# Attention scores: the keys' low parts on 64 rows of TensorE for each head, and one product for both heads in the last block

## The chip, the cores and the metric

The kernel runs on one core of a Trainium2 chip. The metric is the device time of one launch in microseconds (us). TensorE (PE) multiplies, VectorE (DVE), ScalarE (ACT) and GpSimd (POOL) do the elementwise work, SyncE (SP) issues most of the transfers.

## What is computed

Three stages follow one another: a causal attention with a decay, a mixture of four experts over all tokens, and a second mixture in which one of eight experts is picked for some of the tokens. The change is in the first.

```python
def _attn_ref(q, k, v, f):                 # q, k, v: (2, 8, 576, 64), f: (2, 8, 576)
    scores = scale * np.matmul(q, k.transpose(0, 1, 3, 2))
    log_f = np.log(np.clip(f, 0.0001, 1.0))
    cum = np.cumsum(log_f, axis=-1)
    decay = cum[:, :, :, None] - cum[:, :, None, :]
    scores = np.where(causal, -1000000000.0, scores + decay)
    attn = np.exp(scores - np.max(scores, axis=-1, keepdims=True))
    attn = attn / (np.sum(attn, axis=-1, keepdims=True) + 1e-09)
    return np.matmul(attn, v).astype(np.float32)
```

## The kernel before

**Split operands.** A score is made from rounded (fp32r) parts: a head's query q is its rounded value plus the rest, and so is its key k. The 64 features of a head fill only 64 of TensorE's 128 rows. So the host packs q twice, one copy under the other, and the kernel makes of one copy the high part and of the other the low part (`q_low`); the tile is `qa`. One product with the keys' high part `kh`, which also stands on both halves, then gives (q high + q low) times k high. The product of q high with k low needs only the 64 rows of q high. Before, it is run on all 128 rows: the tile `kl` of shape [128, 2, 576] has a head's low part on that head's rows, and zeros on the other 64, which are written once at the start.

**Pairs and steps.** The 16 heads are taken as 8 pairs (p = 0 to 7), and the 576 queries of a head as four blocks of 128 (i = 0 to 3) and a last one of 64, for which both heads of the pair share one block of 128 output rows (i = 4). A pair is thus five steps. `emit_s(p, i)` emits a step's scores: for each head h the product with `kh`, the one with `kl` and the causal mask (a product of a bf16 identity and `maskd`), all into one PSUM tile `s`. N, the columns of a product, is 256, 256, 384 and 512 for i = 0 to 3; block 4 has two halves of 288 columns. DVE then adds the decay and takes the minimum (`sn`, `mn`, L335, or L356 for block 4), ACT takes the exponential (`e`, L338).

**The order is written by hand.** The loop over `steps` (L633) emits for each n in this order: the transposes of the exponentials of step n-2 (`emit_tp`, tiles `tp`, copied to `et` by ACT for head 0 and by DVE for head 1), the scores of step n, for block 4 of the pair before the transposes of the reciprocals of the sums (`emit_rp`, tile `rp`, from `rsx` that ACT writes), and the products with v (`emit_av`, tiles `avm`, `avt`: both heads side by side on 64 columns of TensorE each). Products with v are emitted after the scores of steps i = 1 (28 products, of blocks 2 and 3 of the pair before), i = 2 (block 4 of the pair before) and i = 4 (12 products); after those of steps 0 and 3 the next loop turn's transposes follow at once. In the last two turns there are no scores left, and the first products of the next stage (`early_product`, tiles `p1_e`, `p6_e`, `p7_e`) are emitted among the last pair's remaining work.

**What ties the engines together.** Three PSUM tiles `s` go round. A step takes two, so the second head's tile of step n is the first head's of step n-1: PE waits there until DVE has read that. Each engine takes its instructions in the order in which they are emitted. The splits of the coming pairs (`split_k`: kh on DVE, kl on POOL; `split_q`: qa on DVE, the low part on POOL) are emitted between the steps.

Of the kernel before, what the change touches and what calls it, by code (L numbers as in the profile page):

```python
# [7 lines left out]
F32 = mybir.dt.float32  # L8
# [23 lines left out]
TOPAD = 640  # L32
QW = 2 * TOPAD
# [14 lines left out]
def kernel(  # L48
# [179 lines left out]
    with ExitStack() as at:  # L228
# [7 lines left out]
        ps_s = ps_p[0]  # L236
# [5 lines left out]
        kls = [spl_p.tile([P, 2, S], F32R, tag=f"kl{i}", name=f"kl_{i}", bufs=1) for i in range(2)]  # L242
# [30 lines left out]
        def first_loads():  # L273
            raw = raw_p.tile([P, QKW], F32, tag="raw", name="qk_0")
            state[0] = dict(raw=raw)
            for c0, c1 in ((0, CUT), (CUT, S)):
                for o, st, e in ((QW, S, 0), (0, TOPAD, TOPAD - S)):
                    c2 = c1 + e if c1 == S else c1
                    vw = [x[:, o:o + 2 * st].rearrange("p (h c) -> p h c", h=2)[:, :, c0:c2] for x in (raw, qk[0])]
                    SY.dma_start(out=vw[0], in_=vw[1])  # L280

# [7 lines left out]
        def split_k(p):  # L289
# [8 lines left out]
            for h in range(2):  # L298
                rows = slice(64 * h, 64 * h + 64)
                G.tensor_tensor(out=kl[rows, h], in0=rk[rows, h], in1=kh[rows, h].bitcast(F32), op=ALU.subtract)  # L300

        def q_low(p, h, eng):
            raw, qa = state[p]["raw"], state[p]["qa"]
            rows, cols = slice(64 - 64 * h, 128 - 64 * h), slice(TOPAD * h, TOPAD * h + TOPAD)
# [7 lines left out]
        def emit_s(p, i, between=lambda: None, gaps=None):  # L312
            st = state[p]
            qa, kh, kl, bi = st["qa"], st["kh"], st["kl"], st["bi"]
            if i < 4:
                w = P * (i + 1)
                n = max(256, w)
                pss = []
# [8 lines left out]
                for h in range(2 if gaps else 0):  # L327
                    gaps[h]()
                    q0 = TOPAD * h + i * P
                    T.matmul(out=pss[h][:, :n], lhsT=qa[:, q0:q0 + P], rhs=kl[:, h, :n], start=False, stop=True)  # L330
# [10 lines left out]
            else:  # L341
                sneg = e_p.tile([P, S], F32, tag="sneg", name=f"sn_{p}_t")
                mns = []
                for half in range(2):
                    c0 = half * 288
                    ps = ps_s.tile([P, 512], F32, tag="ps", name=f"s_{p}_t_{half}")
                    for h in range(2):
                        q0 = TOPAD * h + 512
                        T.matmul(out=ps[:, :288], lhsT=qa[:, q0:q0 + P], rhs=kh[:, h, c0:c0 + 288], start=(h == 0),
                                 stop=False)  # L350
                        T.matmul(out=ps[:, :288], lhsT=qa[:, q0:q0 + P], rhs=kl[:, h, c0:c0 + 288], start=False,
                                 stop=(half == 0 and h == 1))
                    if half == 1:
                        T.matmul(out=ps[:, 224:288], lhsT=identb, rhs=maskt, start=False, stop=True)
                    mn = sm_p.tile([P, 1], F32, tag="mn", name=f"mn_{p}_t_{half}")
                    V.tensor_tensor_reduce(out=sneg[:, c0:c0 + 288], in0=ps[:, :288], in1=bi[:, 2, c0:c0 + 288],  # L356
# [134 lines left out]
        def startup():  # L491
# [969 lines left out]
```

## Time and profile before

| | |
|---|---|
| median of 3 runs | 601.87 us (601.19 to 602.26) |
| the profiled execution | 601.63 us, of which the span of the profile is 599.8 us |
| PE | 587.4 us busy (98%), 4027 matmuls |
| DVE, ACT, POOL | 322.1, 266.2, 330.7 us busy |
| attention | from the start to about 111 us |
| granted clock of TensorE | 1.00 from the start to 580 us |

The rows below come from this one execution. A matmul's shown length holds the pipeline's latency, so matmuls overlap in the rows, and what a product occupies of the array is read from start to start.

### The profile page before, as it was taken

What the parts mean: (1) busy time and instruction counts of PE and PEld (TensorE: products, weight loads), DVE (VectorE), ACT (ScalarE), POOL (GpSimd) and SP (SyncE); (2) the same over time, 40 slices, a digit from 0 to 9 for tenths busy, and PEclk for the clock granted to TensorE, in tenths of its full rate; (3) what the DMA queues carried; (4) which work ended last, traced back from release to release, by engine and by line L of the source; (5) the groups of instructions that cost most, each with busy time, mean ns of one, the idle gap of its engine ahead of it and who ended that gap; (6) DMA issues with size and microseconds to landing.
All of it is one profiled execution on the core that took longest, in us unless ns stands there. A gap on an engine that the chain in (4) does not pass through costs nothing. (4 is left out here: it accounts for less than half of the span.)

```text
span 599.8 us, 10818 instructions
## 1 busy us (share of the span) xinstructions
PE 587.4 (98%) x4027; PEld 492.1 (82%) x4027; DVE 322.1 (54%) x820; ACT 266.2 (44%) x675; POOL 330.7 (55%) x378
## 2 busy tenths in 40 slices
PE   8999999999999999999999999999999999999995
PEld 7887778999898898998998989989989775555674
DVE  7988787655453454444534534535436477311483
ACT  8778788674153243344334325315314222112481
POOL 6789978899087178159249339419604143322321
PEclk9999999999999999999999999999999999999998
DMA  7995520321012021011101201202256976999940
GB/s 222 321 338 185 188 95 21 133 71 67 5 71 71 0 72 71 1 58 37 47 12 60 72 0 72 71 0 71 72 210 225 383 256 214 413 418 422 398 158 24
DMA packets 19174, 84.32 MB, mean 141 GB/s; under 512 B 2964, under 2 KB 4000, under 8 KB 11952
## 3 DMA queue, kind: packets, MB, share of 16 engines
q1 hardware_dynamic: 16832, 73.19, 33.8%
q0 software_dynamic: 2288, 10.42, 4.6%
q8 instruction: 32, 0.52, 0.4%
q14 instruction: 22, 0.18, 0.1%
HBM read 79.57 MB, written 5.28 MB: 141 GB/s over the span
## 5 line engine op out<-in xcount | busy, mean ns | idle before, releaser
L914 PE MATMUL dn<-w2h,hh 128*128 128x512 f32 x288 | 114.4, 397 | 0.0
L915 PE MATMUL dn<-w2l,hh 128*128 128x512 f32 x288 | 112.3, 390 | 0.0
L916 PE MATMUL dn<-w2h,hl 128*128 128x512 f32 x288 | 112.2, 390 | 0.0
L926 DVE SCALAR_TENSOR_TENSOR acc<-dn,dps,acc 128x512 f32<-128x512 f32 (+1 forms) x64 | 47.4, 742 | 98.1 <-PE dn L916 97.9
L155 POOL TENSOR_TENSOR w2l<-rawd,w2h 128x512 fp32r<-128x512 f32 x32 | 40.7, 1311 | 94.7 <-ACT w2h L200 94.7
L219 PE MATMUL p<-xb_h,w 128*128 128x320 f32 x224 | 69.2, 309 | 0.0
L218 PE MATMUL p<-xb_l,w 128*128 128x320 f32 x224 | 69.2, 309 | 0.0
L217 PE MATMUL p<-xb_h,w 128*128 128x320 f32 x224 | 69.2, 309 | 0.0
L916 PEld LDWEIGHTS dn<-w2h,hl 128*128 128x128 f32 x288 | 54.1, 188 | 11.5
L914 PEld LDWEIGHTS dn<-w2h,hh 128*128 128x128 f32 x288 | 54.1, 188 | 11.4 <-issue 1.4
L915 PEld LDWEIGHTS dn<-w2l,hh 128*128 128x128 f32 x288 | 54.2, 188 | 9.7
L217 PE MATMUL p<-xa,w 128*128 128x256 f32 x218 | 61.8, 283 | 0.0
L219 PE MATMUL p<-xa,w 128*128 128x256 f32 x218 | 61.7, 283 | 0.0
L218 PE MATMUL p<-xa,w 128*128 128x256 f32 x218 | 61.7, 283 | 0.0
L200 ACT CAST w2h<-rawd 128x512 fp32r<-128x512 f32 x32 | 18.4, 625 | 85.0 <-PE dn L916 85.0
L155 POOL TENSOR_TENSOR hl<-m,hh 128x256 fp32r<-128x256 f32 (+1 forms) x32 | 26.1, 816 | 44.0 <-ACT hh L876 44.0
L870 DVE SCALAR_TENSOR_TENSOR hl<-p,hh 128x320 fp32r<-128x320 f32 (+1 forms) x62 | 28.5, 459 | 35.9 <-ACT hh L869 35.9
L155 POOL TENSOR_TENSOR w<-ws,w 128x512 fp32r<-128x512 f32 x32 | 40.7, 1295 | 3.1 <-ACT w L174 3.1
L217 PEld LDWEIGHTS p<-xb_h,w 128*128 128x128 f32 x224 | 42.1, 188 | 0.3
L218 PEld LDWEIGHTS p<-xb_l,w 128*128 128x128 f32 x224 | 42.1, 188 | 0.3
L217 PEld LDWEIGHTS p<-xa,w 128*128 128x128 f32 x218 | 41.8, 192 | 0.3
L219 PEld LDWEIGHTS p<-xb_h,w 128*128 128x128 f32 x224 | 42.1, 188 | 0.0
(297 smaller groups left out, 1333.8 us busy)
## 6 DMA issues: line engine op xcount, KB each, us to landing
wm<-in_m SPq DMA_DIRECT2D x32, 1024.0 KB, 9.0
rawu<-in_w SPq DMA_DIRECT2D x8, 1024.0 KB, 5.2
rawd<-in_w SPq DMA_DIRECT2D x8, 1024.0 KB
qk<-in_qk SPq DMA_DIRECT2D x7, 640.0 KB, 9.5
qk<-in_qk SPq DMA_DIRECT2D x7, 576.0 KB
bias<-nbd SPq DMA_DIRECT2D x14, 288.0 KB, 6.5
v<-in_v SPq DMA_DIRECT2D x8, 320.0 KB
bias<-nbd SPq DMA_DIRECT2D x16, 144.0 KB, 6.0
```

The costliest lines, as they stand in the source:

```text
L155: eng.tensor_tensor(out=out, in0=a, in1=b, op=ALU.subtract)
L200: A.copy(out=ws["d", u][0][:, c, :], in_=wr["d", u][:, c, :])
L217: T.matmul(out=ps, lhsT=wt[:, 0, a, i, :], rhs=xh[:, i, :], start=(i == 0), stop=False)
L218: T.matmul(out=ps, lhsT=wt[:, 0, a, i, :], rhs=xl[:, i, :], start=False, stop=False)
L219: T.matmul(out=ps, lhsT=wt[:, 1, a, i, :], rhs=xh[:, i, :], start=False, stop=(i == 1))
L870: V.scalar_tensor_tensor(out=hl[:, j, cs], in0=c, scalar=0.0, in1=hh[:, j, cs].bitcast(F32), op0=ALU.max, op1=ALU.subtract)
L914: T.matmul(out=ps, lhsT=hh[:, j, ks], rhs=wh[:, j, :], start=(j == 0), stop=False)
L915: T.matmul(out=ps, lhsT=hh[:, j, ks], rhs=wl[:, j, :], start=False, stop=False)
L916: T.matmul(out=ps, lhsT=hl[:, j, ks], rhs=wh[:, j, :], start=False, stop=(j == 3))
L926: V.scalar_tensor_tensor(out=a, in0=ps[:, c0:c1], scalar=pe, in1=a, op0=ALU.mult, op1=ALU.add)
```

## The change

`kl` becomes [128, 576]: head 0's low part on rows 0 to 63, head 1's on rows 64 to 127, no zeros, and the two writes of zeros go. Its products use 64 rows of `qa` and `kl` each, the heads one after the other. A step's order becomes: kh of both heads, both masks, both products with `kl`. The transposes of `emit_rp`, which came after a step's scores, now come between its masks and its `kl` products (`gaps=turn`); in the last loop turn they come ahead of the early products p6 and p7. For block 4, `qa` gets 128 more columns (QW is 1408, was 1280): the two heads' last 64 queries on a block diagonal, so that one product with `kl` serves both heads; the mask stands ahead of it.

```diff
-TOPAD = 640
-QW = 2 * TOPAD
+QP = 5 * P
+QW = 2 * QP + P
...
-        kls = [spl_p.tile([P, 2, S], F32R, tag=f"kl{i}", name=f"kl_{i}", bufs=1) for i in range(2)]
+        kls = [spl_p.tile([P, S], F32R, tag=f"kl{i}", name=f"kl_{i}", bufs=1) for i in range(2)]
...
+            SY.dma_start(out=raw[:, 2 * QP:QW], in_=qk[0, :, 2 * QP:QW])
...
-        def emit_s(p, i, between=lambda: None, gaps=None):
+        HALVES = (slice(0, 64), slice(64, 128))
+
+        def emit_s(p, i, gaps=lambda: None, between=lambda: None):
...
                 for h in range(2):
-                    ps = ps_s.tile([P, 512], F32, tag="ps", name=f"s_{p}_{i}_{h}")
-                    q0 = TOPAD * h + i * P
-                    T.matmul(out=ps[:, :n], lhsT=qa[:, q0:q0 + P], rhs=kh[:, h, :n], start=True, stop=False)
-                    if not gaps:
-                        T.matmul(out=ps[:, :n], lhsT=qa[:, q0:q0 + P], rhs=kl[:, h, :n], start=False, stop=False)
-                    T.matmul(out=ps[:, i * P:w], lhsT=identb, rhs=maskd, start=False, stop=not gaps)
-                    pss.append(ps)
...
+                    q0 = QP * h + i * P
+                    T.matmul(out=pss[h][:, :n], lhsT=qa[:, q0:q0 + P], rhs=kh[:, h, :n], start=True, stop=False)
+                for h in range(2):
+                    T.matmul(out=pss[h][:, i * P:w], lhsT=identb, rhs=maskd, start=False, stop=False)
+                gaps()
+                for h, rows in enumerate(HALVES):
+                    q0 = QP * h + i * P
+                    T.matmul(out=pss[h][:, :n], lhsT=qa[rows, q0:q0 + P], rhs=kl[rows, :n], start=False, stop=True)
...
+                    if half:
+                        T.matmul(out=pss[1][:, 224:288], lhsT=identb, rhs=maskt, start=False, stop=False)
+                    T.matmul(out=pss[half][:, :288], lhsT=qa[:, 2 * QP:QW], rhs=kl[:, c0:c0 + 288], start=False, stop=True)
...
-            for h in range(2):
-                rows = slice(64 - 64 * h, 128 - 64 * h)
-                V.memset(kls[0][rows, h, :].bitcast(F32), 0.0)
-                A.activation(out=kls[1][rows, h, :], in_=ident[rows, 0:1].to_broadcast([64, S]), func=AF.Copy, scale=0.0)
...
+            V.tensor_copy(out=qa[:, 2 * QP:QW], in_=raw[:, 2 * QP:QW])
...
+            turn = (lambda: emit_rp(lp)) if li == 4 else lambda: None
+            if n < len(steps):
+                emit_s(*steps[n], gaps=turn)
+            else:
+                turn()
             if n == len(steps) + 1:
                 early_product("p6")
                 early_product("p7")
...
+            a[:, h, :, 2 * QP + 64 * h:2 * QP + 64 * h + 64] = qt[:, :, h, 512:576]
```

On PE, step i = 2 of pair 4 reads before as follows (`s_4_2_0` is head 0's scores, `s_4_2_1` head 1's; `identb` is the mask's identity).

```order
L322 MATMUL s_4_2_0_1246<-kh_4_896,qa_4_895 128x384
L324 MATMUL s_4_2_0_1246<-kl_0_145,qa_4_895 128x384
...
L325 MATMUL s_4_2_0_1246<-maskd_143,identb_141 128x128
L322 MATMUL s_4_2_1_1250<-kh_4_896,qa_4_895 128x384
L324 MATMUL s_4_2_1_1250<-kl_0_145,qa_4_895 128x384
...
L325 MATMUL s_4_2_1_1250<-maskd_143,identb_141 128x128
```

In the changed kernel the same place on PE reads:

```order
L325 MATMUL s_4_2_0_1236<-kh_4_888,qa_4_887 128x384
L325 MATMUL s_4_2_1_1237<-kh_4_888,qa_4_887 128x384
...
L327 MATMUL s_4_2_0_1236<-maskd_143,identb_141 128x128
...
L327 MATMUL s_4_2_1_1237<-maskd_143,identb_141 128x128
L331 MATMUL s_4_2_0_1236<-kl_0_145,qa_4_887 128x384
L331 MATMUL s_4_2_1_1237<-kl_0_145,qa_4_887 128x384
```

Head 0's scores end with the fifth product now, where they ended with the third; the last two are those on 64 rows.

At the end of attention PE's order before is this (`tp_7_t` are the last transposes of exponentials, `p6_e`, `p7_e` the early products, `rp_7` the transposes of the last reciprocals, `avm_7` the products with v).

```order
L399 MATMUL tp_7_t1_2048<-ident_78,e_7_t_1999 64x128
L217 MATMUL p6_e_2052<-xa_1_103,w1_0_0_939 128x256
...
L219 MATMUL p7_e_2059<-xa_0_102,w1_0_0_939 128x256
L411 MATMUL rp_7_2066<-ident_78,rsx_7_2025 128x128 x4
L412 MATMUL avt_7_2067<-ident_78,sum_7_1575 128x128
L426 MATMUL avm_7_1896<-et_7_2_0_1975,v_7_1681 64x128
```

And in the changed kernel, the same place:

```order
L400 MATMUL tp_7_t1_2030<-ident_78,e_7_t_1981 64x128
L412 MATMUL rp_7_2034<-ident_78,rsx_7_2007 128x128 x4
L413 MATMUL avt_7_2035<-ident_78,sum_7_1561 128x128
L217 MATMUL p6_e_2045<-xa_1_103,w1_0_0_931 128x256
L218 MATMUL p6_e_2045<-xa_3_105,w1_0_0_931 128x256
```

The twelve early products stood between the last transposes and `rp_7`; now they stand behind it.

## Rows read from the trace of the kernel before

**Rows 1.** The page's first part: busy time, share and instructions of each engine.
```profile
PE 587.4 (98%) x4027; PEld 492.1 (82%) x4027; DVE 322.1 (54%) x820; ACT 266.2 (44%) x675; POOL 330.7 (55%) x378
```

**Rows 2.** Waits, 20 to 112 us: us in total, times, longest.
```profile
DVE et L389 <- PE tp L384: 9.7, 10, 2.0
...
PE s L322 <- DVE mn L335: 2.0, 3, 1.0
```

**Rows 3.** PE's timeline, steps 3 and 4 of pair 4: start, length, instruction.
```profile
63.04 0.48 PE L322 MATMUL s<-kh,qa 128*128 128x512 f32 x1
63.35 0.40 PE L324 MATMUL s<-kl,qa 128*128 128x512 f32 x1
63.59 0.23 PE L325 MATMUL s<-maskd,identb 128*128 128x128 bf16 x1
63.63 0.48 PE L322 MATMUL s<-kh,qa 128*128 128x512 f32 x1
...
64.18 0.23 PE L325 MATMUL s<-maskd,identb 128*128 128x128 bf16 x1
64.25 0.83 PE L384 MATMUL tp<-ident,e 128*128 128x128 f32 x6
...
65.05 0.30 PE L351 MATMUL s_t<-kl,qa 128*128 128x288 f32 x1
65.18 0.29 PE L349 MATMUL s_t<-kh,qa 128*128 128x288 f32 x1
...
65.97 0.20 PE L354 MATMUL s_t<-maskt,identb 128*128 128x64 bf16 x1
66.11 0.88 PE L426 MATMUL avm<-et,v 128*64 128x128 f32 x12
66.91 1.09 PE L384 MATMUL tp<-ident,e 128*128 128x128 f32 x8
67.76 0.37 PE L322 MATMUL s<-kh,qa 128*128 128x256 f32 x1
```

**Rows 4.** PE's timeline, from step 1 of pair 5 to its step 2.
```profile
70.53 0.39 PE L322 MATMUL s<-kh,qa 128*128 128x256 f32 x1 [0.98 <-DVE mn L335]
...
71.31 0.66 PE L411 MATMUL rp<-ident,rsx 128*128 128x128 f32 x4 [0.21 <-ACT rsx L370]
71.81 0.27 PE L412 MATMUL avt<-ident,sum 128*128 128x128 f32 x1
72.01 1.75 PE L426 MATMUL avm<-et,v 128*64 128x128 f32 x28
73.69 0.44 PE L384 MATMUL tp<-ident,e 128*128 128x128 f32 x2
```

**Rows 5.** PE's timeline: the products of the kernel that use 64 rows.
```profile
62.36 0.33 PE L437 MATMUL avt<-et_t,v 64*64 64x64 f32 x4
62.62 0.33 PE L384 MATMUL tp<-ident,e 128*128 128x128 f32 x1
```

**Rows 6.** DVE's timeline, step 3 of pair 4 and step 0 of pair 5.
```profile
63.97 0.69 DVE L335 CUSTOM_DVE_ANT_0 sn<-s,bias 128x512 f32<-128x512 f32 x1 [0.22 <-ACT et L387]
...
70.19 0.28 DVE L335 CUSTOM_DVE_ANT_0 sn<-s,bias 128x128 f32<-128x128 f32 x1
```

**Rows 7.** Timeline of all engines, the last pair's end.
```profile
106.85 0.27 PE L399 MATMUL tp_t<-ident,e_t 128*64 128x128 f32 x1
106.88 0.36 PE L217 MATMUL p_e<-xa,w 128*128 128x256 f32 x1
107.01 0.62 ACT L370 COPY rsx<-sum 128x512 f32<-128x512 f32 x1 [0.82 <-DVE sum L368]
...
108.40 0.60 PE L411 MATMUL rp<-ident,rsx 128*128 128x128 f32 x4
```

**Rows 8.** DVE's timeline at the start: the scan that waits for ACT.
```profile
4.58 0.68 DVE L523 TENSOR_TENSOR_SCAN cum<-one_s,lf 16x256 f32<-16x256 f32 x1 [0.75 <-ACT lf L520]
```

**Rows 9.** Groups of DVE's instructions by line and form, 20 to 110 us.
```profile
L308 DVE CAST qa<-qk 128x1280 fp32r<-128x1280 f32 x6 | 7.4, 1230 | 0.8 <-POOL kl L300 0.8
```

More of the change, by code (lines that the diff above doesn't have):

```diff
@@ L317, in emit_s @@
                 n = max(256, w)
-                pss = []
                 for h in range(2):
-                    ps = ps_s.tile([P, 512], F32, tag="ps", name=f"s_{p}_{i}_{h}")
-                    q0 = TOPAD * h + i * P
-                    T.matmul(out=ps[:, :n], lhsT=qa[:, q0:q0 + P], rhs=kh[:, h, :n], start=True, stop=False)
-                    if not gaps:
-                        T.matmul(out=ps[:, :n], lhsT=qa[:, q0:q0 + P], rhs=kl[:, h, :n], start=False, stop=False)
-                    T.matmul(out=ps[:, i * P:w], lhsT=identb, rhs=maskd, start=False, stop=not gaps)
-                    pss.append(ps)
[L327 to L330, printed above, removed]
+                    q0 = QP * h + i * P
+                    T.matmul(out=pss[h][:, :n], lhsT=qa[:, q0:q0 + P], rhs=kh[:, h, :n], start=True, stop=False)
+                for h in range(2):
+                    T.matmul(out=pss[h][:, i * P:w], lhsT=identb, rhs=maskd, start=False, stop=False)
[3 more added lines that the diff above has]
+                    T.matmul(out=pss[h][:, :n], lhsT=qa[rows, q0:q0 + P], rhs=kl[rows, :n], start=False, stop=True)
                 between()
@@ L345, in emit_s @@
                     c0 = half * 288
-                    ps = ps_s.tile([P, 512], F32, tag="ps", name=f"s_{p}_t_{half}")
                     for h in range(2):
[L348 to L354, printed above, removed]
+                        q0 = QP * h + 512
+                        T.matmul(out=pss[half][:, :288], lhsT=qa[:, q0:q0 + P], rhs=kh[:, h, c0:c0 + 288],
+                                 start=(h == 0), stop=False)
+                    if half:
+                        T.matmul(out=pss[1][:, 224:288], lhsT=identb, rhs=maskt, start=False, stop=False)
+                    T.matmul(out=pss[half][:, :288], lhsT=qa[:, 2 * QP:QW], rhs=kl[:, c0:c0 + 288], start=False, stop=True)
+                for half in range(2):
+                    c0 = half * 288
                     mn = sm_p.tile([P, 1], F32, tag="mn", name=f"mn_{p}_t_{half}")
-                    V.tensor_tensor_reduce(out=sneg[:, c0:c0 + 288], in0=ps[:, :288], in1=bi[:, 2, c0:c0 + 288],
+                    V.tensor_tensor_reduce(out=sneg[:, c0:c0 + 288], in0=pss[half][:, :288], in1=bi[:, 2, c0:c0 + 288],
                                            scale=-0.125, scalar=(3.0e38 if half == 0 else mns[0]),
@@ L582, in startup @@
             SY.dma_start(out=vt, in_=v[0])
[L583 to L585 removed]
+            A.copy(out=sq[:, :, CUT:QP], in_=rq[:, :, CUT:QP])
+            emit_s(0, 0, between=lambda: (bias_mm(P, CUT, P), fill(FILLS[2]), bias_copy(P, CUT, P)))
             for h in range(2):
@@ L633 @@
         for n in range(2, len(steps) + LAG_AV):
+            lp, li = steps[n - LAG_TP] if 0 <= n - LAG_TP < len(steps) else (None, None)
             if n == len(steps) + 1:
                 early_product("p1")
-            if 0 <= n - LAG_TP < len(steps):
-                emit_tp(*steps[n - LAG_TP])
+            if li is not None:
+                emit_tp(lp, li)
                 if n == LAG_TP:
                     fill(FILLS[5])
-                if steps[n - LAG_TP][1] == 3:
-                    emit_inv(steps[n - LAG_TP][0])
+                if li == 3:
+                    emit_inv(lp)
+            turn = (lambda: emit_rp(lp)) if li == 4 else lambda: None
[3 more added lines that the diff above has]
+                turn()
             if n == len(steps) + 1:
@@ L644 @@
                 early_product("p7")
-            lp, li = steps[n - LAG_TP] if 0 <= n - LAG_TP < len(steps) else (None, None)
-            if n < len(steps):
-                p, i = steps[n]
-                emit_s(p, i, (lambda: emit_rp(lp)) if li == 4 else lambda: None)
-            elif li == 4:
-                emit_rp(lp)
             if n >= LAG_AV:
```

30 lines of the change are left out of this document (14 added, 16 removed).

## The prediction

> **What bounds the kernel now.** I read the page first: PE is busy for 98% of the span [rows 1], at full granted clock, and after attention no wait of any length stands ahead of it. A delay of PE in attention is thus a delay of the end. Then the waits [rows 2]: in attention PE does stop, ahead of the second head's product with kh, for DVE to have read a PSUM tile (three times, 2.0 us, longest 0.98), and DVE stops for PE's transposes (ten times, 9.7 us). So the two take turns. PE's timeline shows how [rows 4]: at step 1 of a pair PE waits for DVE's first minimum of step 0; from there PE sets the pace (reciprocals, then 28 products with v, to 73.69), and DVE waits. From the scores of steps 2 and 3 on it is DVE that is late: its reading of step 3 starts at 63.97 and its first of the next pair's step 0 only at 70.19 [rows 6], and PE stands still again.
>
> **Prices, from start to start.** At N = 512 the first product with kh takes 0.31, the one with kl 0.24 (its columns), the mask 0.04 to the next fp32r product [rows 3]. So a product after a mask carries 0.07 of loading weights, one after another fp32r product nothing. At N = 256, 256, 384 the columns cost 0.12, 0.12, 0.18, in proportion; 288 cost 0.13 [rows 3].
>
> Changing how the array is divided costs more. The mask that ends block 4 has 64 columns and still holds off the products with v, which use 64 of the columns of the array, for 0.14, where a full mask holds off the next full product by 0.04 and a transpose by 0.07 [rows 3]; the transpose ahead of the 28 products holds them off by 0.20, where four of its kind take 0.50 [rows 4]. That is about 0.10 more at each entry. Twelve products take 0.80 to the next transpose [rows 3] and 28 take 1.68 [rows 4]: (1.68 - 0.80)/16 = 0.055 each, 0.11 for two that stand side by side, which is the time of one transpose of as many columns (0.85/8 = 0.106 [rows 3]); so such pairs run at the same time. And 0.80 - 6 x 0.11 = 0.14 is left for the first load (0.05) and the way out (0.10). That this holds for a division by rows too: the four products on 64 rows, with half as many columns, take 0.26 from the first to the next transpose [rows 5], not 2 x 0.055; the same 0.15 is over. The Trainium skill has it as a rule ("TensorEngine Tiling (Array Packing)", Key Properties: changing the tiling mode drains TensorE, changing the tile doesn't), and by the rule alone every switch would be paid; the rows agree where a product in another division follows, with the 0.10 above.
>
> **The change on PE.** No product in the trace runs on two row halves side by side. From below, the two kl products take the time of one, as pairs on column halves do; from above, they run one after the other. I take the lower bound, since the pairs of rows 4 are the nearest. Then per step i = 0 to 3:
> - saved: one kl product, 0.12, 0.12, 0.18, 0.24;
> - the loads exposed stay two a step (before: both kh products; now the first kh and the kl pair, whose load of 128 columns shows in full, 0.11 for 0.07);
> - added: the way in, 0.10; and where transposes follow (steps 0 and 3), the way out and their first load, 0.15. Where products with v follow (1 and 2), these were paid before.
>
> So with 0.01 for the second mask: +0.27 - 0.12 = +0.15 (step 0), 0.12 - 0.12 = 0 (step 1), 0.12 - 0.18 = -0.06 (2), 0.27 - 0.24 = +0.03 (3). Block 4 loses two products of 0.13, and the mask that now stands ahead of its last product exposes that one's load (0.04 + 0.07, less the 0.03 it saved at the end): -0.17. The sum over a pair is -0.05; over eight, -0.4. **I count 0.0 on PE**, between -0.4 and +0.4.
>
> **What it does to DVE's turn.** Head 0's scores were ready with the first mask; now they end with the kl pair, behind both kh and both masks. At N = 512 the first mask starts at 0.55 [rows 3]; the last product now starts at 0.31 + 0.24 + 0.05 + 0.15 = 0.75 and ends 0.11 + 0.24 later, where the mask took 0.05: 1.10 against 0.60. PE comes to the step 0.06 earlier (step 2), so DVE gets its first tile of step 3 some 0.45 later. And DVE was waiting for it: it starts at 63.97 [rows 6], 0.15 after the first mask's 63.59 + 0.23 [rows 3]. What is late next is everything that DVE does up to 70.19, and PE's wait at 70.53 with it. Then, after that wait, the transposes of the reciprocals still stand first (they wait for ACT's rsx), and behind them there is now the kl pair with its way in: 0.10 + 0.11 + 0.11, less the kl product and half a mask that stood ahead and were done within the wait for rsx: +0.2 more before the products with v. A round in which PE waits for DVE so grows by about 0.65. There are three such waits [rows 2], 2.0. In the other rounds PE is never long behind DVE, or DVE has some tenths to spare; for two of them I add a quarter each, 0.5 in all, for the rest nothing. **+2.5**, between 0 (DVE has the time) and 8 x 0.65 = 5.2.
>
> **The last pair.** rp_7 now follows the last transposes at once. These start at 106.85, and the next instruction of PE at 106.88; the rsx that rp_7 reads is written by ACT from 107.01 to 107.63 [rows 7]. Before, twelve early products, 106.88 to 108.40, covered that; now PE has nothing else in its queue: 107.65 - 106.88 = **+0.8**. What follows on PE (the next stage's products) was back to back, so nothing gives this back. Bounds: 0.4, if the transposes themselves come later against DVE, and 0.9.
>
> **Start and the rest.** DVE's two writes of zeros and ACT's two go. The first scan waits for ACT's logarithm, 0.75 [rows 8], which stands behind ACT's zeros, so the start may be up to 0.5 earlier; DVE gets a cast of 128 columns there, and the cast of qa grows by a tenth (1.23 for 1280 columns, so 0.12 [rows 9]). In the later pairs that lies in DVE's waits for transposes (9.7 us [rows 2]); without that cover it would be 7 x 0.12 = 0.8. The additional 64 KB for a pair are loaded well ahead. I take **-0.1**, between -0.5 and +0.5.
>
> **Sum.** 0.0 + 2.5 + 0.8 - 0.1 = +3.2 on the profiled execution's own 601.63 (span 599.8 and 1.8 around it): 604.8. The median of the runs is 0.24 higher, less than a measurement tells apart; 0.2%, 1.2 us, is about what it can tell here.
>
> **Rivals.**
> 1. *A division by rows costs no way in or out.* Then a pair saves 0.12 + 0.12 + 0.18 + 0.24 + 0.17 = 0.83 on PE. For it: the lone transpose with 64 weight columns at 106.85 is followed at 106.88 by the next product, with no gap at all [rows 7]. Against it: rows 5. In three rounds that PE sets this gives -2.5; in those that DVE sets, the scores are still some 0.25 late, +0.8; with +0.8 at the end and -0.1: 600.6. If also DVE were never the later one, 8 x -0.83 + 0.7 = 595.7. It ends below the kernel before once the way in and out together cost less than about 0.1. The same page's Theoretical Speedup (up to 2x for 64 rows) would be the full saving of this case if nothing else were paid.
> 2. *The kl pair runs one after the other.* Then a pair takes 0.66 more where PE sets the pace, and 0.3 where DVE does (steps 1 and 2): 3 x 0.66 + 5 x 0.3 = +3.5, 608.3. For it: no such pair in the trace. Against it: the pairs on column halves.
> 3. *DVE has time enough.* Its busy share is 54% [rows 1]; if the late scores fall into its waits, only the last pair's 0.8 less 0.1 is left: 602.3. Against it: DVE starts step 3 right as the scores come.
>
> **Chances.** The forecast 0.55, between 603.2 and 606.5; rival 1 0.17, rival 2 0.13, rival 3 0.15. Faster by over 0.2% (below 600.7): most of rival 1, 0.11. Within 0.2%: the rest of it, most of rival 3 and a little of the forecast, 0.24. Slower: 0.65. The range reaches from rival 1's nearer value to most of rival 2: 600.6 to 607.6.
>
> **What would show it.** In the changed kernel's profile: a kl pair (L331) 0.15 or so after the second mask, both within 0.02 of each other, and the next operation 0.10 beyond its columns (right), or a mask followed by it in 0.04 (rival 1), or the second a whole product later (rival 2). PE's waits for DVE's minimum above 2.0 us and DVE's first `sn` of step 3 later against its kh product by 0.45 (right), or no longer (rival 3). rp_7 with a wait of 0.7 for ACT's rsx. I am wrong if the attention ends before 111 us, or if pairs lengthen where neither engine waits.

## The result and the profile after

| | before | after |
|---|---|---|
| median | 601.19 us (5 runs, 600.56 to 602.26) | 606.38 us (5 runs, 605.28 to 607.08) |
| ratio | | 1.008, 95% interval 1.0061 to 1.0099 |
| profiled execution, its span | 601.63, 599.8 us | 606.92, 605.1 us |
| end of attention | 111.45 us | 115.33 us |

The change costs 5 us. The end of attention is here, and for every run below, the start of PE's first product `p` of the next stage behind the last `avt` product. It comes 3.88 us later. The rest of the difference between the two profiled executions, 1.4 us, lies far behind the change, as the clock shows further down. The 3.88 compares one execution with one. Behind attention the kernel before takes 488.35 us in its profile (the profiles below without a dip of the clock there 488.05 to 488.71), but the shortest of its executions measured beside the experiments have spans of 598.7 to 599.0 us, so in those attention ended about 1 us earlier (an estimate: 598.9 - 488.35 = 110.5). The 3.88 may be too small by that much; by the ratio the change costs 4.8 us (3.7 to 6.0).

The page's first part, which answers [rows 1]:

```profile
PE 590.2 (98%) x4011; PEld 486.5 (80%) x4011; DVE 319.2 (53%) x819; ACT 264.0 (44%) x673; POOL 331.4 (55%) x378
```

Sixteen matmuls fewer, and PE is busy 2.8 us longer. The waits of the stretch 20 to 112 us (total, times, longest) answer [rows 2]:

```profile
DVE sn L336 <- PE s L331: 12.0, 15, 1.3
...
DVE et L390 <- PE tp L385: 5.2, 10, 1.3
...
PEld s L325 <- DVE mn L336: 3.2, 6, 0.9
...
PEld rp L412 <- ACT rsx L371: 2.2, 8, 1.1
...
PE s L325 <- DVE mn L336: 2.0, 5, 0.7
...
PEld tp L385 <- ACT et L388: 1.5, 7, 0.3
...
PE tp_t L396 <- DVE et L390: 1.1, 6, 0.2
```

The lines of the kernel before to set beside them:

```profile
PEld s L322 <- DVE mn L335: 2.6, 4, 1.1
...
DVE sn L335 <- PE s L325: 1.9, 8, 0.2
...
PEld tp L384 <- ACT et L387: 0.8, 4, 0.3
...
PE tp_t L395 <- DVE et L389: 0.2, 1, 0.2
```

DVE now waits for the scores themselves, 12.0 us; before, the list has 1.9 us for that. Of the 12.0, 7.2 lie in step 1 of the pairs, where the transposes of the reciprocals stand ahead of the kl products. But PE's own wait for DVE's minimum is 2.0 us still, in five parts instead of three (the waits of its weight loads for it are 3.2 instead of 2.6). What PE lost must lie elsewhere: the last two lines of either list, waits in front of transposes, grew, and the step lengths below show where they stand.

PE's timeline of the same place as [rows 3], steps 3 and 4 of pair 4:

```profile
64.41 0.72 PE L325 MATMUL s<-kh,qa 128*128 128x512 f32 x2
64.97 0.28 PE L327 MATMUL s<-maskd,identb 128*128 128x128 bf16 x2
65.19 0.50 PE L331 MATMUL s<-kl,qa 64*128 64x512 f32 x2
65.62 0.87 PE L385 MATMUL tp<-ident,e 128*128 128x128 f32 x6
66.25 0.52 PE L349 MATMUL s<-kh,qa 128*128 128x288 f32 x2
...
67.04 0.38 PE L353 MATMUL s<-kl,qa 128*128 128x288 f32 x1
67.35 0.88 PE L427 MATMUL avm<-et,v 128*64 128x128 f32 x12
68.16 1.31 PE L385 MATMUL tp<-ident,e 128*128 128x128 f32 x8
69.22 0.49 PE L325 MATMUL s<-kh,qa 128*128 128x256 f32 x2
```

The two kl products take 0.43 together up to the next operation. Block 4 lasts 66.25 to 67.35, 1.10. The eight transposes of step 3's exponentials take 1.06 (68.16 to 69.22), where they took 0.85 in [rows 3]: PE waits in the middle of them.

DVE's timeline there, which answers [rows 6]:

```profile
65.83 0.69 DVE L336 CUSTOM_DVE_ANT_0 sn<-s,bias 128x512 f32<-128x512 f32 x1 [0.39 <-ACT et L388]
```

DVE's first reading of step 3 starts 1.42 after the first kh product (65.83 - 64.41); before, 63.97 - 63.04 = 0.93. So head 0's scores are 0.49 later. (The profile puts the end of this wait down to ACT in some pairs and to PE in others, but DVE starts 1.42 to 1.43 behind the kh product in every pair from pair 2 on, and 0.93 before.)

ACT goes on from there. Its exponentials and, behind them in its order, the copy `et` of the transposes of step 2, then the weight loads of PE's last four transposes:

```profile
66.57 0.73 ACT L339 ACTIVATE e<-sn,mn 128x512 f32<-128x512 f32 x1 [0.76 <-DVE mn L336]
...
68.29 0.47 ACT L388 COPY et<-tp 128x384 f32<-128x384 f32 x1
```

```profile
68.81 0.42 PEld L385 LDWEIGHTS tp<-ident,e 128*128 128x128 f32 x4 [0.23 <-ACT et L388]
```

And ACT before:

```profile
64.70 0.73 ACT L338 ACTIVATE e<-sn,mn 128x512 f32<-128x512 f32 x1 [0.74 <-DVE mn L335]
...
66.43 0.47 ACT L387 COPY et<-tp 128x384 f32<-128x384 f32 x1
```

Counted from the first kh product, the copy ends at 4.35 (68.76 - 64.41) instead of 3.86 (66.90 - 63.04), again 0.49 later, and PE's transposes, which start earlier than before on this count, run into it: the loads of the last four start 0.05 after its end.

The end of the last pair, all engines, which answers [rows 7]:

```profile
109.72 0.27 PE L400 MATMUL tp_t<-ident,e_t 128*64 128x128 f32 x1
...
110.13 0.62 ACT L371 COPY rsx<-sum 128x512 f32<-128x512 f32 x1 [0.82 <-DVE sum L369]
...
110.80 0.66 PE L412 MATMUL rp<-ident,rsx 128*128 128x128 f32 x4 [0.81 <-ACT rsx L371]
```

PE stands still for 0.81 ahead of rp_7.

**Step lengths.** The table is worked out from starts: from a step's first kh product to that of the next step, mean over pairs 1 to 6; "least" is the shortest such step in which PE waits for nothing long, the least of pairs 1 to 6 (for step 1 it comes from the two runs with the cast on ACT, below, where PE's wait for DVE is nearly gone).

| step | before, mean | least | after, mean | least |
|---|---|---|---|---|
| 0 | 1.32 | 1.23 | 1.57 | 1.38 |
| 1 | 3.93 | 3.27 | 4.02 | 3.34 |
| 2 | 2.42 | 2.37 | 2.32 | 2.31 |
| 3 | 1.91 | 1.79 | 1.95 | 1.83 |
| 4 | 2.93 | 2.93 | 2.89 | 2.75 |
| pair | 12.51 | 11.59 | 12.76 | 11.61 |

PE's own work is the same in both kernels, 11.6 us for a pair. Before, a pair takes 0.92 more than that, after 1.15. Step 1, with the wait for DVE's minimum, hardly grew. What grew is the part above the least in steps 0 (0.09 to 0.19) and 4 (0.00 to 0.14), both of them in front of transposes of exponentials.

**The clock.** Windows of the changed kernel behind attention (busy time and instructions of each engine, granted clock, DMA share, GB/s), and of the same work before:

```profile
498.00:502.80 4.80, 4.57 (x35) 3.71 (x33) 2.62 (x15) 1.10 (x3) 0.88 (x4) 1.00 0.39 122
502.80:506.40 3.60, 3.60 (x18) 1.77 (x18) 1.38 (x7) 0.00 (x0) 0.00 (x0) 0.53 0.88 350
506.40:510.00 3.60, 3.60 (x27) 2.23 (x29) 2.13 (x16) 1.52 (x13) 1.09 (x1) 1.00 0.52 218
```

```profile
498.80:502.40 3.60, 3.53 (x30) 2.57 (x30) 2.89 (x18) 0.00 (x0) 0.00 (x0) 1.00 0.88 337
```

From 502.8 to 506.4 the granted clock is 0.53, which is the 1.2 GHz level; before it, PE had been busy 4.57 of 4.80 us at 1.00. In the stretch PE gets through 18 matmuls, where the kernel before gets through 30. From the first `xsel` product to the first `up` product it takes 5.73 us instead of 4.18: +1.55, and that is the rest of the difference. Such a dip falls into some executions whatever the change (the profiles of e4 and e5 below have one too), so the experiments below are compared by the end of attention and by ratios over several runs.

### The profile page after: what moved, and what is told of

Its sections match the earlier page's. It is cut to its first block, busy times and chain, and to the rows that moved or that the text cites. A ratio compares the mean times of both kernels' runs of the same rounds, so it can differ in the third digit from the quotient of the medians.

```text
span 605.1 us, 10787 instructions
## 1 busy us (share of the span) xinstructions
PE 590.2 (98%) x4011; PEld 486.5 (80%) x4011; DVE 319.2 (53%) x819; ACT 264.0 (44%) x673; POOL 331.4 (55%) x378
## 5 line engine op out<-in xcount | busy, mean ns | idle before, releaser
L217 PEld LDWEIGHTS p<-xb_h,w 128*128 128x128 f32 x224 | 42.0, 188 | 0.3
L217 PEld LDWEIGHTS p<-xa,w 128*128 128x128 f32 x218 | 41.8, 192 | 0.3
L218 PEld LDWEIGHTS p<-xa,w 128*128 128x128 f32 x218 | 41.8, 192 | 0.3
```

Of the source, the lines that this page charges most:

```text
L217: T.matmul(out=ps, lhsT=wt[:, 0, a, i, :], rhs=xh[:, i, :], start=(i == 0), stop=False)
L218: T.matmul(out=ps, lhsT=wt[:, 0, a, i, :], rhs=xl[:, i, :], start=False, stop=False)
```

## The experiments

The runs side by side. The end of attention is that of the profiled execution, and the three columns behind it take it apart: where pair 1 starts (its first kh product), how long pairs 1 to 6 take, and from there to the end of attention. Ratios are to the kernel before on the same chip.

| run | end of attention, us | pair 1 starts | pairs 1 to 6 | last pair | median, us | ratio (95%) |
|---|---|---|---|---|---|---|
| before | 111.45 | 18.29 | 75.03 | 18.13 | | |
| after | 115.33 | 18.60 | 76.56 | 20.18 | 606.38 | 1.008 (1.0061 to 1.0099) |
| e1_early_first | 114.40 | 18.57 | 76.70 | 19.13 | 604.69 | 1.0052 (1.0032 to 1.0073) |
| e2_order_alone | 112.30 | 18.56 | 74.95 | 18.79 | 602.94 | 1.002 (1.0005 to 1.0035) |
| e3_rp_after_scores | 113.95 | 18.85 | 76.14 | 18.96 | 603.54 | 1.004 (1.0025 to 1.0055) |
| e4_before_act_cast | 110.02 | 18.83 | 73.09 | 18.10 | 601.59 | 0.999 (0.9976 to 1.0004) |
| e5_after_act_cast | 116.43 | 20.85 | 75.28 | 20.30 | 607.0 | 1.0085 (1.0063 to 1.0107) |
| e6_kl_rows_in_place | 121.76 | 18.62 | 83.12 | 20.03 | 611.66 (one run) | |
| e7_block4_alone | 123.69 | 33.39 | 72.18 | 18.12 | 614.76 | 1.0217 (1.0201 to 1.0233) |
| e8_block4_act_cast | 123.82 | 33.20 | 72.53 | 18.09 | 615.61 | 1.0232 (1.0213 to 1.0251) |
| e9_block4_start_mended | 118.34 | 19.37 | 80.88 | 18.10 | 607.85 | 1.0118 (1.009 to 1.0145) |
| e10_late_mask | 112.58 | 18.50 | 75.29 | 18.79 | 603.3 | 1.0035 (1.0021 to 1.005) |
| e11_block4_from_pair2 | 110.86 | 19.29 | 73.47 | 18.10 | 602.12 | 1.001 (1.0001 to 1.0019) |
| e12_late_mask_same_work | 113.26 | 18.52 | 75.83 | 18.91 | 604.31 | 1.0048 (1.0034 to 1.0062) |

How far one execution can be trusted shows in pair 0, which has the same instructions in the changed kernel, e1 and e3: pair 1 starts at 18.60, 18.57 and 18.85. So a few tenths between two ends of attention say nothing by themselves.

**e1_early_first.** The changed kernel with the early products back in front:

```diff
+            if n == len(steps) + 1:
+                early_product("p6")
+                early_product("p7")
             if n < len(steps):
                 emit_s(*steps[n], gaps=turn)
             else:
                 turn()
-            if n == len(steps) + 1:
-                early_product("p6")
-                early_product("p7")
```

> The changed kernel, with the early products p6 and p7 back ahead of rp_7. Theory (three causes: late scores that hold up DVE, 2.5 us; rp_7 without cover, 1.0 us; the start, 0.3 us): PE's wait of 1.08 us ahead of rp_7 is gone, the first product after attention starts at 114.3 instead of 115.3 us, and the time is 1.0 us under the changed kernel's, about 604.3 to 605.4. Rival (nothing is lost there, the wait only moves to the products with v): 115.3, no change.

Attention ends 0.93 earlier than in the changed kernel. PE's timeline at the place of [rows 7], from the lone transpose over the twelve products to rp_7:

```profile
109.81 0.27 PE L400 MATMUL tp_t<-ident,e_t 128*64 128x128 f32 x1
109.84 0.36 PE L217 MATMUL p_e<-xa,w 128*128 128x256 f32 x1
...
111.24 0.28 PE L219 MATMUL p_e<-xa,w 128*128 128x256 f32 x1
111.36 0.60 PE L412 MATMUL rp<-ident,rsx 128*128 128x128 f32 x4
```

No wait is left. The last pair's term stands, at 0.93.

**e3_rp_after_scores.** e1, and the transposes of the reciprocals after a step's scores again:

```diff
-                emit_s(*steps[n], gaps=turn)
+                emit_s(*steps[n], between=turn)
```

> The changed kernel with two places of its order put back: the early products p6 and p7 ahead of the last reciprocals' transposes (as in the run e1_early_first), and the transposes of the reciprocals after a step's scores instead of between its masks and its kl pair. Theory (late scores): the four transposes of rp and the one beside them, 0.7 us in all, no longer stand ahead of the kl pair of step 1, so its scores are ready that much earlier, and the kl pair hides its way in within the wait for ACT's rsx; a round in which PE then waits for DVE gives back about 0.2: attention ends at 113.0 to 113.9 us (114.40 in e1_early_first), time 603.3 to 604.2. Rival (the place of the reciprocals' transposes does not matter, since DVE has step 0 to read at that time): attention ends at 114.2 to 114.6, time as e1_early_first, 604.7.

113.95: 0.45 earlier than e1, 0.05 outside the theory's interval and nearer to it than to the rival's; counted from the start of pair 1 it is 0.73. Step 1 goes from 4.02 to 3.88 (worked out as above). So the place of rp costs something, but less than the 0.2 a round that the prediction counted. DVE's wait for the scores falls far more than that:

```profile
DVE sn L336 <- PE s L331: 7.2, 14, 0.7
```

It was 12.0, so 4.8 us less of waiting on DVE gave back 0.45 to 0.73.

**e2_order_alone.** The kernel before, all on 128 rows, with the order kh, kh, mask, mask, kl, kl (of steps 0 and 1 of pair 0 before) in every step:

```diff
-                    if not gaps:
-                        T.matmul(out=ps[:, :n], lhsT=qa[:, q0:q0 + P], rhs=kl[:, h, :n], start=False, stop=False)
-                    T.matmul(out=ps[:, i * P:w], lhsT=identb, rhs=maskd, start=False, stop=not gaps)
                     pss.append(ps)
-                for h in range(2 if gaps else 0):
-                    gaps[h]()
+                for h in range(2):
+                    T.matmul(out=pss[h][:, i * P:w], lhsT=identb, rhs=maskd, start=False, stop=False)
+                for h in range(2):
+                    if gaps:
+                        gaps[h]()
```

> The kernel before, with the changed order of a step alone: kh of both heads, both masks, both kl, all on 128 rows, block 4 and the rest untouched. No switch of the array's division is added; head 0's scores are ready some 0.35 us later at 512 columns. Theory (late scores cost time): attention ends 0.8 to 1.5 us later than before (111.4), 602 to 602.7. Rival (the switches cost the time on PE, lateness costs nothing): 111.4, 601.2, no change.

+0.85. Here head 0's scores come 0.35 later in step 3 and 0.28 in step 2 (DVE's first reading against the first kh product), where the change makes them 0.49 and 0.43 later. The order alone costs, without a division by rows: the ratio's interval stays above 1. By the columns of the table the 0.85 lies in pair 0 (0.27) and in the last pair (0.66), and pairs 1 to 6 take no longer than before.

**e10_late_mask and e12_late_mask_same_work.** The kernel before with only the end of head 0's scores moved: in e10 its whole mask goes behind head 1's products; in e12 only the last 64 of its 128 columns do, so that PE has no less work than before. First e10, then e12:

```diff
-                    T.matmul(out=ps[:, i * P:w], lhsT=identb, rhs=maskd, start=False, stop=not gaps)
                     pss.append(ps)
+                    if gaps:
+                        T.matmul(out=ps[:, i * P:w], lhsT=identb, rhs=maskd, start=False, stop=False)
+                for h in range(0 if gaps else 2):
+                    T.matmul(out=pss[1 - h][:, i * P:w], lhsT=identb, rhs=maskd, start=False, stop=True)
```

```diff
-                    T.matmul(out=ps[:, i * P:w], lhsT=identb, rhs=maskd, start=False, stop=not gaps)
                     pss.append(ps)
+                    if gaps:
+                        T.matmul(out=ps[:, i * P:w], lhsT=identb, rhs=maskd, start=False, stop=False)
+                    else:
+                        c = w if h else w - 64
+                        T.matmul(out=ps[:, i * P:c], lhsT=identb, rhs=maskd[:, 0:c - i * P], start=False, stop=(h == 1))
+                if not gaps:
+                    T.matmul(out=pss[0][:, w - 64:w], lhsT=identb, rhs=maskd[:, 64:P], start=False, stop=True)
```

> The kernel before with head 0's mask moved behind head 1's products and mask in steps 0 to 3 (kh, kl, kh, kl, mask, mask; steps 0 and 1 of pair 0 as before). All products on 128 rows, as many as before; PE's own work is 0.05 less in a step. Head 0's scores now end with the step, at N = 512 some 0.5 later, as in the changed kernel (e2_order_alone had about half of that). Theory (what costs is how late head 0's scores are): attention ends 1.5 to 2.7 us later than in the kernel before, at 113.0 to 114.1, time 603.4 to 604.5. Rival (what costs in the changed kernel is the division by rows, as work of PE): attention ends at 111.0 to 112.3, time 601.4 to 602.8.

> e10_late_mask with PE's work put back to that of the kernel before: head 0's mask is split, its first 64 columns stay in the old place, between the heads, and only the last 64 columns come behind head 1's products (one more product of 64 columns in a step, no division changed). Head 0's scores end as late as in e10. Theory (lateness costs, and e10 hid part of its price behind 0.05 to 0.07 less work of PE in a step): attention ends 0.5 to 1.5 us later than in e10 (112.58), at 113.1 to 114.1, near the changed kernel with its two places of order put back (113.95 in e3_rp_after_scores), time 603.4 to 605. Rival (lateness costs only what e10 showed, and the division by rows the rest): attention ends at 112.3 to 112.9, time as e10, 603.3.

e10 came to +1.13, between the two expectations; e12 to +1.81, at the low end of the theory's. Neither has quite the work of the kernel before: the least lengths of steps 0, 2 and 3 (1.23, 2.37, 1.79 before) are 1.15, 2.29, 1.78 in e10 and 1.28, 2.40, 1.85 in e12, together 0.17 less and 0.14 more. Between the two, at equal work, lateness costs about 1.5 us (an estimate: 1.13 + 0.68 x 0.17/0.31). By the ratios it is 2.1 us in e10 (1.3 to 3.0) and 2.9 in e12 (2.0 to 3.7), of 4.8 for the change. Step 3 of pair 4 in e12, PE and then DVE:

```profile
63.41 0.48 PE L322 MATMUL s<-kh,qa 128*128 128x512 f32 x1
...
64.62 0.19 PE L332 MATMUL s<-maskd,identb 128*128 128x64 bf16 x1
64.65 0.85 PE L390 MATMUL tp<-ident,e 128*128 128x128 f32 x6
...
67.34 1.25 PE L390 MATMUL tp<-ident,e 128*128 128x128 f32 x8
68.36 0.36 PE L322 MATMUL s<-kh,qa 128*128 128x256 f32 x1
```

```profile
64.96 0.69 DVE L341 CUSTOM_DVE_ANT_0 sn<-s,bias 128x512 f32<-128x512 f32 x1 [0.51 <-PE s L332]
```

DVE starts 1.55 after the first kh product (1.45 in e10, 1.42 in the changed kernel), and the eight transposes of step 3 take 1.02 instead of 0.85, much as in the changed kernel (1.06). Half a mask in another place, with no division changed and 0.14 more work in a pair, brings 1.81 of the 3.88 us.

**e6_kl_rows_in_place.** The kernel before, with each kl product on its head's 64 rows, at its old place:

```diff
-                        T.matmul(out=ps[:, :n], lhsT=qa[:, q0:q0 + P], rhs=kl[:, h, :n], start=False, stop=False)
+                        rows = slice(64 * h, 64 * h + 64)
+                        T.matmul(out=ps[:, :n], lhsT=qa[rows, q0:q0 + P], rhs=kl[rows, h, :n], start=False, stop=False)
```

> The kernel before with one thing changed: in steps 0 to 3 each head's product with kl takes its head's 64 rows alone, and stays where it was, between the head's product with kh and its mask (the zeros are still written, block 4 is as before). No order changes and no two stand side by side, so it prices the change of division alone. Theory (way in 0.10 and a load of 128 columns exposed, 0.11; way out 0.10 and the mask's load): at N = 512 kh to kl 0.52 (0.31 before), kl to mask 0.34 to 0.40 (0.24 before); 0.3 to 0.37 for each of some 60 products, of which PE's waits absorb a part: attention ends at 122 to 131 us (111.45 before), time 612 to 621. Rival (a division by rows costs no way in or out): distances as before, 0.31 and 0.24, attention ends at 111.5 and the time is that of the kernel before, 601.9.

Its PE timeline at a step 3:

```profile
54.88 0.47 PE L322 MATMUL s<-kh,qa 128*128 128x512 f32 x1
55.29 0.50 PE L325 MATMUL s<-kl,qa 64*128 64x512 f32 x1
55.72 0.23 PE L326 MATMUL s<-maskd,identb 128*128 128x128 bf16 x1
55.76 0.47 PE L322 MATMUL s<-kh,qa 128*128 128x512 f32 x1
```

From kh to kl 0.41 where [rows 3] has 0.31 (0.405 against 0.315 in the trace's nanoseconds), from kl to the mask 0.43 where it has 0.24. So a change there and back costs 0.09 + 0.19 = 0.28. The sum agrees: a pair takes 13.85 us in this run, step by step the same in every pair from pair 1 on, and (13.85 - 11.59)/8 = 0.28. Attention ended at 121.76, just below the expected 122 to 131, since the price is 0.28 and not 0.3 to 0.37. Rival 1 falls.

**e4_before_act_cast and e5_after_act_cast.** Both kernels with the cast of kh, 0.83 on DVE, on ACT:

```diff
-            V.tensor_copy(out=kh, in_=rk)
+            A.copy(out=kh, in_=rk)
```

> The kernel before, with the cast of kh (1.0 to 1.3 us a pair) moved from DVE to ACT in pairs 1 to 7. Theory: DVE is what PE waits for at step 1 of a pair, so these waits (2.0 us) go and attention ends 1 to 2 us earlier, about 599.5; it serves as the base of the next run. If ACT becomes late instead (it is busy for four fifths of attention), the time rises.

> The changed kernel with the same cast moved to ACT. Theory (2.5 of the 3.9 us come from DVE getting its scores late): with DVE relieved in both, the changed kernel's attention ends only 1.3 to 2 us after that of the run before this one, instead of 3.9. Rival (PE's own work grew by the switches): the distance stays at 3.9 us.

The kernel before gained 1.43 in attention (and no ratio that a measurement tells from 1), the changed one lost 1.10, so the distance is 6.4: neither expectation. About 2 us of it are a clock dip in the profile of e5 at 15.3 to 18.7 us: its pair 1 starts at 20.85 instead of 18.60. Counted from the start of pair 1, both kernels gain by the cast on ACT, 1.97 and 1.15, and the distance grows from 3.57 to 4.39 instead of shrinking: pairs 1 to 6 take 75.28 against 73.09. The waits of e5, 20 to 112 us:

```profile
DVE sn L336 <- PE s L331: 13.2, 16, 1.3
...
PEld tp_t L400 <- ACT et L388: 3.2, 5, 0.8
...
PE tp_t L400 <- ACT et L388: 2.0, 5, 0.5
```

In both kernels step 1 falls to its least (3.32 before, 3.38 after on the mean of pairs 1 to 6), so the wait for DVE's minimum is gone. And step 0 grows, from 1.32 to 1.75 before and from 1.57 to 2.06 after: PE then waits in front of block 4's transposes, behind ACT. The theory that DVE alone holds the late scores is wrong. They pass down a chain, scores, minimum, exponential, and the copy `et` that stands behind the exponentials in ACT's order and for which PE's next transposes wait. With DVE relieved, part of the wait only moved to the end of that chain.

**e7_block4_alone, e8_block4_act_cast, e9_block4_start_mended, e11_block4_from_pair2.** The part of the change that saves work, alone: one kl product for both heads in block 4, all on 128 rows, in the order of before. `kl` is packed as in the change; the zeros stand in `qz`, a copy of q's high parts that transfers on the chip fill from `qa` (`q_alone`; `EARLY_Q` and `LATE_Q` name the columns that are copied first and later).

```diff
+        qz = spl_p.tile([P, 2 * TOPAD - P], F32R, tag="qz", name="qz", bufs=1)
...
+        def q_alone(p, *cuts):
+            qa = state[p]["qa"].bitcast(F32)
+            for h, o, c0, c1 in cuts:
+                rows = slice(64 * h, 64 * h + 64)
+                SY.dma_start(out=qz[rows, o + c0:o + c1].bitcast(F32), in_=qa[rows, TOPAD * h + c0:TOPAD * h + c1])
...
-                        T.matmul(out=ps[:, :n], lhsT=qa[:, q0:q0 + P], rhs=kl[:, h, :n], start=False, stop=False)
+                        T.matmul(out=ps[:, :n], lhsT=qz[:, q0:q0 + P], rhs=kl[:, :n], start=False, stop=False)
...
-                        T.matmul(out=ps[:, :288], lhsT=qa[:, q0:q0 + P], rhs=kl[:, h, c0:c0 + 288], start=False,
-                                 stop=(half == 0 and h == 1))
+                    T.matmul(out=ps[:, :288], lhsT=qz[:, 512:TOPAD], rhs=kl[:, c0:c0 + 288], start=False, stop=True)
...
```

> The one part of the change that saves work on PE, alone: block 4's low parts in one product of a block diagonal, with every product on all 128 rows and in the order of the kernel before. kl is packed as in the changed kernel; the zeros stand in a copy of q's high parts instead (a tile that transfers on the chip fill from qa, 8 pairs of them). Only steps 0 and 1 of the first pair take 64 rows. Theory (block 4 saves 0.17 on PE in each pair): attention ends 0.6 to 1.3 us earlier than in the kernel before, at 110.2 to 110.9 (the less where DVE sets the pace), time 600.6 to 601.3. Rival a (the saving is lost in PE's waits for DVE): 111.4, 601.9. Rival b (PE waits for the additional transfers): PE waits for a DMA stand in the list, attention ends after 112.

> e7_block4_alone with the cast of kh on ACT in place of DVE, as in e4_before_act_cast. Theory (the two gains add, since the one relieves DVE and the other PE): attention ends 0.8 to 1.3 us earlier than in e4_before_act_cast (110.02), at 108.7 to 109.2, time 599.0 to 600.2 where no clock dip falls. Rival (both take the same wait away): 109.8 to 110.2, time as e4_before_act_cast, 600.2 to 601.6.

The edit of e8 beside it is that of e4. Both miss at the start, by e7's rival b: PE waited 12.5 us (e8: 12.2) in pair 0 for the first transfers into `qz`, which stood in SP's queue behind the loads of pair 1 (in e7 these landed up to 24.35, the three transfers at 24.88 to 25.22). From pair 1 to pair 7 e7 took 72.18 us (33.39 to 105.57) against 75.03, e8 72.53, so the cast on ACT adds nothing to it.

In e9 the first pair does without the transfers:

```diff
-            q_alone(0, *LATE_Q)
...
+            for h in range(2):
+                V.tensor_copy(out=qz[64 * h:64 * h + 64, 512:TOPAD], in_=qa[64 * h:64 * h + 64, TOPAD * h + 512:TOPAD * h + TOPAD].bitcast(F32))
...
-                emit_s(p, i, (lambda: emit_rp(lp)) if li == 4 else lambda: None)
+                emit_s(p, i, (lambda: emit_rp(lp)) if li == 4 else lambda: None, None if p else (lambda: None,) * 2)
```

> e7_block4_alone without the transfers for the first pair, for which PE waited 12.5 us there: all four steps of pair 0 take 64 rows for kl, in the order of the changed kernel, and DVE writes the block diagonal of pair 0 (two copies of 64 rows and 128 columns). From pair 1 on it is e7_block4_alone. Theory (block 4's saving holds, and PE and DVE meet less often): pairs 1 to 6 take 72.2 us as there (75.03 in the kernel before, 33.39 to 105.57 there), pair 0 as in the changed kernel to 18.6, the last pair 18.1: attention ends at 108.9, time 599.3. Rival (the pairs were short there because DVE, POOL and the loads had got ahead in the first pair's wait): only block 4's 0.17 in each pair is left, attention ends at 110.2 to 110.8, time 600.6 to 601.2.

Again a miss, by the same mechanism in pair 1 (transfers issued from 18.12 on landed from 25.43 on, behind loads that landed up to 25.23), in the waits of 5 to 45 us:

```profile
PE s L334 <- DMA qz<-qa: 5.7, 1, 5.7
```

In e11 pair 1 does without them too:

```diff
-                emit_s(p, i, (lambda: emit_rp(lp)) if li == 4 else lambda: None, None if p else (lambda: None,) * 2)
+                emit_s(p, i, (lambda: emit_rp(lp)) if li == 4 else lambda: None, None if p > 1 else (lambda: None,) * 2)
...
-                    q_alone(1, *EARLY_Q)
...
-                if i == 4 and nx:
+                if p and i == 4 and nx:
...
+                    for h in range(2):
+                        V.tensor_copy(out=qz[64 * h:64 * h + 64, 512:TOPAD], in_=state[1]["qa"][64 * h:64 * h + 64, TOPAD * h + 512:TOPAD * h + TOPAD].bitcast(F32))
```

> e9_block4_start_mended with the transfers for pair 1 taken away as well (PE waited 5.7 us for one of them there): pairs 0 and 1 take 64 rows for kl in the order of the changed kernel, DVE writes both their block diagonals, and the transfers on the chip begin with pair 2. Theory: pairs 0 and 1 as in the changed kernel, to 30.9; pairs 2 to 6 as in e9, 61.0 us (62.55 in the kernel before); the last pair 18.1: attention ends at 110.0, time 600.3, 1.5 us below the kernel before. Rival (the shorter pairs of e7 and e9 were due to DVE and POOL being ahead after PE's long wait): pairs 2 to 6 take 61.9 to 62.6, attention ends at 110.9 to 111.6, time 601.3 to 602.

Here the queue is out of the way (1.2 us of such waits are left), and pairs 2 to 6 take 60.89 (31.87 to 92.76), against 62.55 before: the theory's 61.0, and no effect of PE's long wait. Its rival is out. Block 4's step is 2.75 in every pair, 0.18 less; that is 0.9 of the 1.66 in these five pairs, and where the rest comes from was not followed. But pairs 0 and 1, on 64 rows, end 1.1 later than before, not 0.1, so attention ends only 0.59 earlier, and the median, 602.12 against 601.44, shows no gain. The saving stands in pairs 2 to 6, and is too small to pay for this start. No version here beats the kernel before by more than its measurement can tell.

## Why the prediction was right, and which of its steps were not

The time, 606.38, lies in the range, and slower was forecast with 0.65. The profiled execution was to go from 601.63 to 604.8, by 3.2; without the dip's 1.55 it went to 605.4, by 3.7. By the ratio the change costs 4.8 (3.7 to 6.0), so the sum was rather low.

**PE's own work, forecast 0.0: right.** By the table of least lengths: +0.15 in step 0 (forecast +0.15), +0.07 in step 1 (0), -0.06 in step 2 (-0.06), +0.04 in step 3 (+0.03), -0.18 in block 4 (-0.17); +0.02 a pair. Two kl products on the two row halves run at the same time: 0.43 for two of them in the changed kernel, and 0.43 for one in e6. Rival 2 falls with that. The sign that was named came out: the kl products start 0.15 behind the second mask and 0.003 apart; only the next operation comes 0.19 beyond their columns (0.43 - 0.24) and not 0.10. And a change of division is paid: 0.28 there and back in e6, where the forecast had 0.10 and 0.10 and loads of 0.05 and 0.11. The rule of the Trainium skill that it weighed ("TensorEngine Tiling (Array Packing)", Key Properties: a change of the tiling mode drains TensorE) agrees with e6; the page has no figure for it. In the changed kernel steps 0 and 3 pay it whole, steps 1 and 2 only the way in, since the way to the products with v was paid before too; that eats up what the products save (step 0: 0.28 - 0.12 = 0.16, measured 0.15; step 3: 0.28 - 0.24 = 0.04, measured 0.04).

**Late scores, forecast +2.5: the size about right, the place wrong.** Head 0's scores came 0.49 later, where 0.45 was forecast. From the start of pair 1 to the end, the changed kernel takes 96.73 us (18.60 to 115.33), the kernel before 93.16; less the last pair's 0.93 that is +2.6, of which 0.1 is PE's own work. But the step said that PE's waits for DVE's minimum grow by 0.65 a round, and they did not: 2.0 us before and after, step 1 longer by 0.09. The time went to PE's waits in front of transposes instead, in steps 4 and 0: where it waits for the copies `et` of the transposes before, in step 4 for ACT's and in step 0 for DVE's (1.5 and 1.1 us in the lists above), since these stand behind the exponentials and come later as well. The step that failed is "what is late next is everything that DVE does up to 70.19, and PE's wait at 70.53 with it": it followed DVE, and not ACT behind it. That the sum came out is partly luck: three rounds with 0.65 were priced, and six pairs paid 0.25 each and the last one 1.0 (19.13 in e1 against 18.13), 0.6 of it in its step 0. Rival 3 (DVE has time) falls with e2, e10 and e12; the 54% that it rested on is the mean of all three stages, and in pairs 1 to 6 of the kernel before DVE is busy for 62.1 of 75.0 us. Lateness alone is 1.1 to 1.8 by e10 and e12, in all pairs together (2.1 and 2.9 by their ratios).

**The last pair, forecast +0.8:** 0.93 by e1; the wait for rsx was 0.81.

**The start, forecast -0.1: wrong in sign.** In the three executions with the changed pair 0 and no dip in it, pair 1 starts at 18.57, 18.60 and 18.85, against 18.29 in the one of the kernel before. The first scores start at 5.88 against 6.34, but that is not shown to be the change's: e1, with the same start, has 6.78. The kh product of head 1 in step 0 stands right behind head 0's in PE's queue now, and waits there 0.37 for its q. I did not follow how the rest of pair 0 came about.

Put in a row, the runs take the 3.88 us apart: 111.45, then about 112.95 with the late scores alone (the estimate between e10 and e12, +1.5), 113.95 with the divisions, block 4's product and the changed start as well (e3, +1.0, of which pair 0 has 0.33: pair 1 starts at 18.85, in e12 at 18.52), 114.40 with rp between masks and kl (e1, +0.45), 115.33 with the early products behind rp_7 (+0.93). Each part is the difference of single executions. Counted from the start of pair 1, without pair 0 and its spread, the row is 93.16, about 94.4 (+1.3), 95.10 (+0.7), 95.84 (+0.73) and 96.73 (+0.90). The +0.7 to +1.0 was not taken apart further, so what the divisions cost beside lateness, if anything, stays open.

## What to carry to other kernels

When products are put side by side to save columns, look first at when the first of the outputs is ready, not only at the sum on TensorE: here the sum stayed at 11.6 us a pair, and half a microsecond of lateness in one PSUM tile of a step cost 1.1 to 1.8 us of attention in e10 and e12. A delay is to be followed through every engine of the chain, down to the next instruction of TensorE that reads its end; relieving one engine of it moves part of the wait (in e4 and e5 step 1 lost 0.6 in the mean pair, and step 0 grew by 0.4 to 0.5). And work that stands in a queue between a wait and what it waits for is cover: twelve early products moved behind that wait cost 0.93 us.

## What the runs showed of the hardware that was not expected

**A long wait of PE costs more than itself.** In e7, PE stands still from 12.5 to 25.0 us. The windows:

```profile
14.00:17.00 3.00, 0.00 (x0) 0.00 (x0) 0.00 (x0) 0.00 (x0) 1.00 (x1) 1.00 1.05 274
17.00:20.00 3.00, 0.00 (x0) 0.00 (x0) 0.00 (x0) 0.00 (x0) 0.00 (x0) 0.51 1.01 396
...
25.00:30.00 5.00, 4.98 (x18) 3.45 (x19) 3.13 (x9) 2.37 (x7) 1.73 (x2) 0.50 0.08 19
...
31.00:34.00 3.00, 3.00 (x32) 2.57 (x30) 2.74 (x11) 2.03 (x6) 0.59 (x5) 1.00 0.25 54
```

The granted clock falls to 0.5 (1.2 GHz) during the wait and is still there for 5 us in which PE is busy throughout: 18 matmuls in 5 us, against 32 in 3 us afterwards. In e9 the same follows on a wait of 5.7 us. So in e7 and e9 a transfer that came late was paid for again in the slow stretch behind the wait.

**The price of a change of division is uneven.** In e6 it is 0.09 into the products on 64 rows and 0.19 out of them, at N = 256 (kh to kl 0.29 against 0.20, kl to mask 0.31 against 0.12) as at N = 512, although what follows is only a mask in bf16.
